# Extra matmuls in the first attention batch, and the gate/value weights' float32 words moved a part behind their halves

## The chip, the core and the metric

One core of a Trainium2 chip runs the whole program. TensorE (PE) multiplies, VectorE (DVE), ScalarE (ACT) and GpSimd (POOL) do the elementwise work, SyncE (SP) issues every DMA. The metric is device time in microseconds, median of 3 runs.

## What is computed

Attention over 4 batches, 8 heads, 576 positions of 64, in two forms that are added; then a gated block and a squared-ReLU block over 2304 tokens.

```python
q_d, k_d, v_d = means of 4 neighbouring positions
out = repeat(sm_attn(q_d, k_d, v_d), 4) + softmax(scale*q@k.T where |i-j| < 4) @ v
x = out as (2304, 512)
xn = x / sqrt(mean(x*x) + 1e-6) * rms_g
x = (silu(xn @ w_gate) * (xn @ w_val)) @ w_out        # 512 -> 1536 -> 512
h = relu(x @ w_in)
y = (s*h*h + b) @ w_out2                              # 512 -> 2048 -> 512
```

The weights come as 64-bit floats, the rest as 32-bit floats.

## The kernel before

A planner (the tile framework) lays out each engine's instructions at build time: it takes instructions by a priority, which follows the order in which the code emits them and can be shifted (`high_priority`), and by a simulated clock. On the chip each engine takes its own list in that order. `issue_after(ins)` makes what is emitted inside it follow `ins` on that engine's list.

**Stages.** Batch 0 of attention runs first, as four units of two heads each (`early_unit`), then the gated block for token blocks 0 and 1 of 288 (`main01`) with attention batch 1 beside it, then the other blocks with batches 2 and 3, then the second block of layers. `attn_batch` starts a new unit of batch 0 every second step and runs `norm` for each half of the batch behind it; the norm's results X16 are what the gate/value products read.

**A unit.** `load_unit` issues nine DMAs on SP. For batch 0 the rows of q and k lie six to a partition; later batches have one row per partition and chunk. `early_unit` turns q and k (L423 for batch 0: a matmul with the identity for each head and chunk; L426 for the others: one transpose for both heads), ACT copies them out of PSUM (L428), then come local scores `sl` with the mask added by a matmul (L440, L444), scores of the means `sd` (L461), softmaxes on DVE and ACT, turns of the weights (`tpl`, `tpd`), and value products `pvd` and `pl`. `sl`, `sd`, `pvd`, `pl` and the turned tiles are each a PSUM tile.

**Weights.** `rest()` emits the preparation of the gated block's weights in steps: for each of four parts (`prep_gv`) eight chunks of 128 x 384, four of w_gate and four of w_val, then two maxima (`st`, L646, L647), scales, and two groups of splits into half-precision pairs. A chunk is fetched by one DMA into staging (`fetch`, L621) and converted to float32 words by two passes on ACT (L624, L625) and two on DVE (L626, L630). The split by DVE (`halves`) is one ACT and one DVE instruction (L127, L128); that by POOL is two POOL instructions with one of ACT between (L130, L131, L132). w_gate is split with DVE, w_val with POOL. After the parts, `weigh` fetches the twelve chunks of w_out, squares them (L666), sums the squares by a matmul `so` (L671), and splits them.

**Where they lie.** `Chain` keeps the words of a chunk 512 columns behind the place of its halves in `W1`, so the halves of one chunk lie on words of the two chunks before it. `Cgv` starts at column 0, `Co` (w_out) at 12288. Staging has four places in `W1` from column 14720 (`ring`), which 28 fetches may use, and two of its own. The loads of three units of batch 0 also lie in `W1`, at 11776, 6656 and 9216.

**Order by hand.** `queued(1)` puts part 1's instructions on ACT and DVE behind the second local softmax of unit 3 (`gates[1]`), `queued(2)` those of parts 2 and 3 and of w_out behind the first half's norm (`gates[2]`). SP, PE and POOL have no such gate. In `main01` each step of the products asks `rest_it` for two further steps; a step of `moe1_gv` is 12 matmuls (`pg` or `pvl`, L708). What `rest_it` has left is emitted before `moe1_out` (`po`, L729).

Of the kernel before, what the change touches and what calls it, by code (L numbers as in the profile page):

```python
# [8 lines left out]
F32 = mybir.dt.float32  # L9
F16 = mybir.dt.float16  # L10
BF16 = mybir.dt.bfloat16
I32 = mybir.dt.int32
# [6 lines left out]
B, H, S, D = 4, 8, 576, 64  # L19
NT, DM, F1, F2 = 2304, 512, 1536, 2048  # L20
NP = H // 2
KC = DM // 128
NF1 = F1 // 128
# [5 lines left out]
GR = 96  # L29
# [10 lines left out]
REST = 2  # L40
RATE0 = 0
EARLY = 2
CAP0 = 100
PDPE = 2
DEP = False
# [1 line left out]
MASKB = 1  # L47
LOADW = (0, 1, 1, 1)
PIN = 0
RING = 4  # L50
RINGN = 28
RESTN = 1
OFF = 0
OFF1 = 0
# [15 lines left out]
def kernel(  # L70
# [46 lines left out]
    Xf = X.rearrange("p k g c -> p k (g c)")  # L117
    X16 = X.bitcast(F16).rearrange("p k g (h c) -> p k g h c", h=2)

    ENG = [(dve, pool)] * NPART + [dve]  # L120

    QB = (dve, dve)
    DEM = pool if DEP else dve
# [28 lines left out]
        def split(self, o, n, scale, eng):  # L152
            halves(self.half(o, n, 0), self.half(o, n, 1), self.f32(o, n), scale, eng)

    Cgv = Chain(W1, 0, 512)
    Co = Chain(W1, 12288, 512)
    C3 = Chain(W1, 0, 512)

# [72 lines left out]
    def load_unit(b, hp, qkf, vd, vw):  # L231
        h0 = 2 * hp
        for t, src in enumerate((q, k)):
            for h in range(2):
                if b == 0:
                    sp.dma_start(out=qkf[:, t, h], in_=src[b, h0 + h].rearrange("(p c) d -> p c d", c=6))
                else:
                    sp.dma_start(out=qkf[:, t, :, h, :], in_=src[b, h0 + h].rearrange("(c p) d -> p c d", p=GR))
        sp.dma_start(out=vd.rearrange("p a r d -> p a (r d)"),
                     in_=v[b, h0:h0 + 2].rearrange("h (t p r) d -> p (h t) (r d)", p=72, r=4))  # L240
        sp.dma_start(out=vw[:, :, 0, :], in_=v[b, h0:h0 + 2, 0:WIN, :].rearrange("h p d -> p h d"))
        sp.dma_start(out=vw[:, :, 8, :], in_=v[b, h0:h0 + 2, S - WIN:S, :].rearrange("h p d -> p h d"))
        for h in range(2):
            base = v[b, h0 + h, 61:62, 0:1]
            sp.dma_start(out=vw[:, h, 1:8, :],
                         in_=bass.AP(tensor=base.tensor, offset=base.offset, ap=[[D, WIN], [64 * D, 7], [1, D]]))
# [94 lines left out]

    LL = ((0, 0), (0, 1), (1, 0))

    def values_d(vdh, PdT, scale, pairs=LL):
        pvd = pV.tile([128, SD], F32, tag="v", name="pvd")
        n_ = 2 * len(pairs) - 1
        for sl, c0, a0, n in ((0, 0, 0, 64), (1, 64, 0, 64), (2, 128, 48, 16)):
            i = 0
            for g in range(2):
                for lv, lp in pairs:  # L350
                    for h in range(2):
                        pe.matmul(out=pvd[64 * h:64 * h + 64, c0:c0 + n], lhsT=vdh[:, lv, 2 * h + g, :],  # L352
                                  rhs=PdT[:72, 6 * lp + 2 * sl + g, 64 * h + a0:64 * h + a0 + n],
                                  start=i == 0, stop=i == n_, skip_group_check=True)
                    i += 1
        od = ap.tile([128, SD], F32, tag="od", name="od", bufs=2)
        act.activation(out=od, in_=pvd, func=AF.Copy, scale=scale)
        return od

    def values_l(b, hp, js, vh, PlT, od, scale, pairs=LL):  # L360
        pl = pV.tile([128, 320], F32, tag="v", name="pl")
        for j in js:
            o = 64 * (j - js[0])
            for i, (lv, lp) in enumerate(pairs):
                for h in range(2):
                    ph = slice(64 * h, 64 * h + 64)
                    pe.matmul(out=pl[ph, o:o + 64], lhsT=vh[:, lv, h, j, :],  # L367
                              rhs=PlT[:WIN, 9 * lp + j, ph], start=i == 0, stop=i == len(pairs) - 1,
                              skip_group_check=True)
        lo, n = 64 * js[0], 64 * len(js)  # L370
        t0 = b * S
        dve.scalar_tensor_tensor(
            out=Xf[:, hp, t0 + lo:t0 + lo + n].rearrange("p (a r) -> p a r", r=4),
            in0=pl[:, :n].rearrange("p (a r) -> p a r", r=4), scalar=scale,
            in1=od[:, lo // 4:(lo + n) // 4].unsqueeze(2).to_broadcast([128, n // 4, 4]),
            op0=ALU.mult, op1=ALU.add)
# [10 lines left out]

    JS = (range(5), range(5, 9))

    def turned(b, n, name):  # L390
        if b == 0:
            return mmp.tile([128, 3, n], F32, tag="mm", name=name)
        return pS.tile([128, 3, n], F32, tag="s", name=name)

    def early_unit(b, hp, sq_sum):
# [17 lines left out]
        qkT = st["qkT"]  # L413
        for t in range(2):
            qT = qkT[:, S * t:S * t + S]
            qT = qT.rearrange("p (a c) -> p c a", c=6) if b == 0 else qT.rearrange("p (c a) -> p c a", c=6)
            for g in range(2):
                tp = turned(b, GR, "tp")
                for i in range(3):
                    c = 3 * g + i  # L420
                    if b == 0:
                        for h in range(2):
                            pe.matmul(out=tp[64 * h:64 * h + 64, i, :], lhsT=qkf[:, t, h, c, :],  # L423
                                      rhs=ident_f[:GR, :GR], start=True, stop=True, skip_group_check=True)
                    else:
                        pe.transpose(out=tp[:, i, :], in_=qkf[:, t, c].rearrange("p h d -> p (h d)"),  # L426
                                     identity=ident_f[:GR, :GR])
                act.activation(out=qT[:, 3 * g:3 * g + 3, :], in_=tp, func=AF.Copy)  # L428
        q4 = qkT.rearrange("p (a r) -> p a r", r=4)
        q2 = st["PlT"][:, :576].rearrange("p (a r) -> p a r", r=2)  # L430
# [5 lines left out]

        def local(js):
            sl = pS.tile([128, 5, WIN], F32, tag="s", name="sl")
            for p0 in (0, 64):
                pe.matmul(out=sl[p0:p0 + 64, :len(js), :], lhsT=ident_b[p0:p0 + 64, p0:p0 + 64],  # L440
                          rhs=mask[p0:p0 + 64, js[0]:js[0] + len(js), :], start=True, stop=False, skip_group_check=True)
            for j in js:
                for p0 in (0, 64):
                    pe.matmul(out=sl[p0:p0 + 64, j - js[0], :], lhsT=qkT[p0:p0 + 64, 64 * j:64 * j + 64],  # L444
                              rhs=qkT[p0:p0 + 64, S + win0(j):S + win0(j) + WIN], start=False, stop=True,
                              skip_group_check=True)
            return sl
# [8 lines left out]

        sl = local(JS[0])
        sd = pX.tile([128, 3, SD], F32, tag="x", name="sd")
        for o, q0 in ((0, 0), (1, 64), (2, SD - 64)):
            for p0 in (0, 64):  # L460
                pe.matmul(out=sd[p0:p0 + 64, o, :], lhsT=qd[p0:p0 + 64, q0:q0 + 64],  # L461
                          rhs=qd[p0:p0 + 64, SD:2 * SD], start=True, stop=True, skip_group_check=True)
# [16 lines left out]
            act.activation(out=PdT[:72, 3 * g:3 * g + 3, :], in_=tp[:72], func=AF.Copy)  # L479
        a = p1.tile([128, TB], F32, tag="u", name="a1", bufs=3)[:, :280].rearrange("p (j k) -> p j k", j=4) if b == 0 else None  # L480
        a = softmax_l(sl, JS[1], 1.0 / 8, 1.0, 1, dve if b == 0 and hp == NP - 1 else pool, a)
        if b == 0 and hp == NP - 1:
            gates[1] = tuple(last)
        yield
        od = values_d(vs.unsqueeze(1), PdT, 0.25, ((0, 0),))
        turn(a, JS[1])
        yield
        values_l(b, hp, JS[0], vw.unsqueeze(1), PlT, od, 1.0, ((0, 0),))
# [77 lines left out]
    def norm(b, hh, sq_sum):  # L566
# [28 lines left out]
            last[:] = (act.activation(out=dst[:, :, 0, :], in_=sv, func=AF.Copy).ins,  # L595
                       eng.tensor_tensor(out=dst[:, :, 1, :], in0=sv, in1=dst[:, :, 0, :], op=ALU.subtract).ins)
        if b == 0 and hh == 0:
            gates[2] = tuple(last)
        yield


    ring = [W1[:, 14720 + 1024 * i:14720 + 1024 * i + 1024].bitcast(I32).rearrange("p (n t) -> p n t", t=2)
            for i in range(RING)]
    fetched = [0]

# [198 lines left out]
    def rest():  # L804
        for p_ in range(NPART + 1):
            it = prep_gv(p_, ENG[p_]) if p_ < NPART else weigh(Co, w_out, NF1, 0, invg, ENG[4], "o")
            while True:
                with queued(min(p_, 2)) if p_ else nullcontext():
                    if next(it, 0) == 0:
                        break  # L810
                yield

    late = [LATE0]

    def later_rest():
        it = rest()
        while True:
            with tc.high_priority(offset=-late[0]):
                if next(it, 0) == 0:
                    return  # L820
            yield

    rest_it = later_rest()
    staged = []
    for hp in range(NP):
        o = (11776, 6656, 9216, 0)[hp]
        if hp < NP - 1:
            st_ = (W1[:GR, o:o + 1536].rearrange("p (t h c d) -> p t h c d", t=2, c=6, h=2),
                   W1[:72, o + 1536:o + 2560].rearrange("p (a r d) -> p a r d", a=4, r=4))
        else:  # L830
            st_ = (ap.tile([GR, 2, 2, 6, D], F32, tag="qkf", name="qkf"),
                   ap.tile([72, 4, 4, D], F32, tag="vd", name="vd"))
        st_ += (early[hp]["vh"][:WIN].rearrange("p (h j d) -> p h j d", h=2, j=NJ),)
        for _ in range(LOADW[hp]):
            next(rest_it)
        load_unit(0, hp, *st_)
        staged.append(st_)
# [47 lines left out]
    for blk in range(NB):  # L885
# [31 lines left out]
        for n, ev_ in enumerate(main(blk) if blk else main01()):  # L917
            if blk == 0:
                if n % RESTN == 0:
                    for _ in range(REST):  # L920
                        next(rest_it, None)
            if n == 1 or ev_ == "post":
                run_posts()
            if side is not None:
# [123 lines left out]
```

## Time and profile before

| | us |
|---|---|
| median of 3 runs | 1107.35 (1106.99 to 1108.79) |
| the profiled execution | 1106.15 |
| its span | 1104.4 |
| PE busy | 1003.6 (91%) |
| DVE, ACT, POOL busy | 592.8, 521.4, 339.5 |

The trace is of one execution. Times in it run from the span's start. [...] A matmul's duration holds its passage through the array, so matmuls that follow each other closely add up to more than the time they take together; the "busy" of a stretch counts such overlap once.

### The profile page before, as it was taken

Reading aid. Unit: us, or ns where it says so; the run is one execution under the profiler, and the core shown is the slowest. Engines: PE = TensorE matmul, PEld = TensorE weight load, DVE = VectorE, ACT = ScalarE, POOL = GpSimd, SP = SyncE. Lnnn points to the kernel's source line nnn. Section 1 sums busy time; section 2 is a strip of 40 time slices with the busy share of each in tenths; the row PEclk is TensorE's granted clock in tenths of the full one; section 3 lists DMA queues with packets and bytes.
Section 4 is the critical chain, followed back from the end, with each engine's and each line's share of the span. In section 5 each row is a group of like instructions: output and inputs, shape, how many; then the busy total and the mean of one; then the engine's idle time right before and its main releaser. Section 6 shows DMA issues by size and latency. Waiting matters only on the chain.

```text
span 1104.4 us, 20466 instructions
## 1 busy us (share of the span) xinstructions
PE 1003.6 (91%) x8204; PEld 685.4 (62%) x8206; DVE 592.8 (54%) x1255; ACT 521.4 (47%) x1174; POOL 339.5 (31%) x433
## 2 busy tenths in 40 slices
PE   5775686899988989898999999999999999999998
PEld 4663564678866767676778667755554545455553
DVE  3766996642187764576762876656341414234241
ACT  3655778643255554355644777756140413223140
POOL 6435674246144545453644213621000000000000
PEclk7675885899988989998999999999999999999999
DMA  8733456100035542145511442400000000000000
GB/s 195 212 87 98 137 156 174 36 20 13 1 67 91 116 88 49 39 84 90 117 38 39 134 134 77 160 32 1 29 1 29 1 20 11 10 20 1 29 1 29
DMA packets 120431, 73.59 MB, mean 67 GB/s; under 512 B 102161, under 2 KB 108305, under 8 KB 120337
## 3 DMA queue, kind: packets, MB, share of 16 engines
q1 hardware_dynamic: 120336, 72.29, 26.1%
q8 instruction: 64, 1.05, 0.4%
q14 instruction: 31, 0.25, 0.1%
HBM read 54.97 MB, written 4.72 MB: 54 GB/s over the span
## 4 chain that ended last, share of the span: by engine, by line
PE 66%; DMA 13%; DVE 10%; ACT 6%; issue 3%; POOL 2%; SPq 1%; DVEq 0%; POOLq 0%; ACTq 0%
PE y L1010 17%; PE ph L990 16%; PE po L729 8%; PE pvl L708 8%; PE pg L708 8%; DMA stg<-in_moe_w_in_dram 3%; DMA qkT<-qk 3%; DMA stg<-in_moe_w_out_dram 2%; DVE W L630 2%; DVE stg L626 2%; DMA vd<-in_v_dram 2%; ACT stg L625 1%; PE pl L367 1%; PE pvd L352 1%; ACT W L624 1%
## 5 line engine op out<-in xcount | busy, mean ns | idle before, releaser
L708 PEld LDWEIGHTS <-W 128*128 128x128 f16 x2304 | 229.1, 101 | 88.9 <-issue 23.9
L990 PE MATMUL ph<-X,W 128*128 128x384 f16 x1152 | 196.6, 326 | 0.4 <-DVE s4o L673 0.3
L708 PE MATMUL pg<-X,W 128*128 128x288 f16 x1152 | 170.2, 296 | 15.0 <-DVE u L715 11.0
L708 PE MATMUL pvl<-X,W 128*128 128x288 f16 x1152 | 172.3, 295 | 0.6 <-DVE m L647 0.5
L990 PEld LDWEIGHTS <-W 128*128 128x128 f16 x1152 | 112.6, 98 | 81.5 <-issue 1.2
L1010 PE MATMUL y<-W 128*128 128x512 f16 x648 | 151.6, 379 | 0.0
L729 PEld LDWEIGHTS <-W 128*128 128x128 f16 x1152 | 111.5, 98 | 31.1 <-issue 2.8
L729 PE MATMUL po<-g,W 128*128 128x288 f16 x1008 | 129.0, 287 | 1.6 <-DVE u L715 0.9
L994 ACT ACTIVATE r<-ph 128x384 f32<-128x384 f32 x96 | 47.0, 490 | 175.8 <-PE ph L990 126.1
L719 POOL TENSOR_TENSOR g<-u,g 128x288 f16<-128x288 f32 x84 | 72.1, 859 | 140.3 <-ACT g L718 106.1
L1010 PEld LDWEIGHTS <-W 128*128 128x128 f16 x648 | 63.4, 98 | 70.9
L190 DVE SCALAR_TENSOR_TENSOR r<-ph,r 128x384 f32<-128x384 f32 x96 | 53.5, 557 | 59.5 <-ACT r L994 59.5
L1015 DVE SCALAR_TENSOR_TENSOR ys<-y,ccol,bcol 128x512 f32<-128x512 f32 x18 | 13.5, 751 | 121.1 <-PE y L1010 118.9
L718 ACT ACTIVATE g<-u 128x288 f16<-128x288 f32 x84 | 36.8, 438 | 77.7 <-DVE u L190 72.6
L715 DVE SCALAR_TENSOR_TENSOR u<-u,pvl 128x288 f32<-128x288 f32 x96 | 42.7, 447 | 45.7 <-PE pvl L708 42.2
L626 DVE SCALAR_TENSOR_TENSOR stg<-stg 128x512 int32<-128x512 int32 (+1 forms) x56 | 42.3, 756 | 35.0 <-ACT stg L625 34.4
L998 DVE TENSOR_TENSOR W<-r,W 128x384 f16<-128x384 f32 x72 | 40.1, 557 | 36.6 <-ACT W L997 36.6
L997 ACT ACTIVATE W<-r 128x384 f16<-128x384 f32 x72 | 37.5, 521 | 39.9 <-DVE r L190 39.9
L714 ACT ACTIVATE u<-pg,tsc 128x288 f32<-128x288 f32 x96 | 47.1, 492 | 16.5 <-PE pg L708 15.7
L1010 PE MATMUL y<-W,r2b 128*128 128x512 f16 x216 | 50.0, 379 | 0.0
L630 DVE SCALAR_TENSOR_TENSOR W<-W,stg 128x512 int32<-128x512 int32 (+1 forms) x56 | 47.9, 857 | 2.9 <-ACT W L624 2.3
L624 ACT ACTIVATE W<-stg 128x512 f32<-128x512 f32 (+1 forms) x56 | 36.0, 645 | 21.0 <-DMA stg<-in_moe_w_out_dram 10.0
(260 smaller groups left out, 1462.1 us busy)
## 6 DMA issues: line engine op xcount, KB each, us to landing
stg<-in_moe_w_out_dram SPq DMA_DIRECT2D x28, 512.0 KB
stg<-in_moe_w_in_dram SPq DMA_DIRECT2D x16, 512.0 KB
W<-in_moe_w_gate_dram SPq DMA_DIRECT2D x12, 384.0 KB
out_dram<-ys SPq DMA_DIRECT2D x18, 256.0 KB
qkf<-in_q_dram SPq DMA_DIRECT2D x26, 144.0 KB
qkf<-in_k_dram SPq DMA_DIRECT2D x26, 144.0 KB
vd<-in_v_dram SPq DMA_DIRECT2D x13, 288.0 KB
W<-in_moe_w_val_dram SPq DMA_DIRECT2D x8, 384.0 KB
```

The costliest lines, as they stand in the source:

```text
L190: (eng or dve).scalar_tensor_tensor(out=o, in0=a, scalar=s, in1=b, op0=ALU.mult, op1=ALU.mult)
L624: act.activation(out=dst, in_=stg[:, :, 1].bitcast(F32), func=AF.Copy, scale=2.0 ** -112)
L626: ins = dve.scalar_tensor_tensor(out=stg[:, :, 0], in0=stg[:, :, 1], scalar=-2 ** 31, in1=stg[:, :, 0], op0=ALU.bitwise_and, op1=ALU.bitwi ...
L630: dve.scalar_tensor_tensor(out=di, in0=di, scalar=3, in1=stg[:, :, 0], op0=ALU.logical_shift_left, op1=ALU.bitwise_or)
L708: pe.matmul(out=acc, lhsT=Cgv.half(o, FP, lw)[:, f0 * 128:f0 * 128 + 128], rhs=X16[:, kc, 3 * blk:3 * blk + 3, lx, :], start=i == 0, stop= ...
L714: act.activation(out=u, in_=ps[0], func=AF.Tanh, scale=tsc[:, part:part + 1])
L715: dve.scalar_tensor_tensor(out=u, in0=u, scalar=1.0, in1=ps[1], op0=ALU.add, op1=ALU.mult)
L719: pool.tensor_tensor(out=lo, in0=u, in1=hi, op=ALU.subtract)
L729: pe.matmul(out=acc, lhsT=Co.half(fc * 512, 512, lw)[:, m * 128:(m + 1) * 128], rhs=g16(fc)[:, lx, :], start=i == 0, stop=i == 35)
L990: pe.matmul(out=acc, lhsT=C2.half((p * KC + kc) * 512, 512, lw)[:, f0 * 128:f0 * 128 + 128], rhs=X16[:, kc, 4 * blk:4 * blk + 4, lx, :], s ...
L994: act.activation(out=r, in_=acc, func=AF.Relu, scale=2.0 ** -23)
L1010: pe.matmul(out=y, lhsT=src[:, lx, tt * 128:(tt + 1) * 128], rhs=C3.half(fc * 512, 512, lw), start=i == 0, stop=i == 47)
```

## The change

- Batch 0 (`WARMB = 1`) gets matmuls whose results nobody reads: after each allocation of a PSUM tile of a unit, `warm` multiplies a matrix of ones by the mask into that tile, 2, 2, 2, 4 or 2 times (turned tiles, `sl`, `sd`, `pvd`, `pl`). The real matmuls then overwrite it.
- The shift of `Cgv` grows from 512 columns to 3072, the words of one part. Staging moves to column 15744, has three places, and 37 fetches may use it.
- Parts 0 and 1 split w_val with DVE instead of POOL.
- Batch 0 loads and turns q and k as the other batches do.
- `gates[1]` is unit 1's second local softmax, `gates[2]` unit 3's, `gates[3]` the norm; part p waits for gate p, w_out for gate 3.
- In `main01` the loop asks for no more than 60 steps of `rest_it` (four parts of 12 and the 12 fetches of w_out).

```diff
+WARMB = 1
+WARM = (2, 2, 2, 4, 2)
-RING = 4
-RINGN = 28
+RING = 3
+RINGN = 37
-    ENG = [(dve, pool)] * NPART + [dve]
+    ENG = [(dve, dve), (dve, dve), (dve, pool), (dve, pool), dve]
-    Cgv = Chain(W1, 0, 512)
+    Cgv = Chain(W1, 0, FP * 8)
@@ load_unit
-                if b == 0:
-                    sp.dma_start(out=qkf[:, t, h], in_=src[b, h0 + h].rearrange("(p c) d -> p c d", c=6))
-                else:
-                    sp.dma_start(out=qkf[:, t, :, h, :], in_=src[b, h0 + h].rearrange("(c p) d -> p c d", p=GR))
+                sp.dma_start(out=qkf[:, t, :, h, :], in_=src[b, h0 + h].rearrange("(c p) d -> p c d", p=GR))
@@ values_d, values_l, local and the tile sd likewise
+            warm(warm_b, pvd, WARM[3])
+        warm(b, pl, WARM[4])
+            warm(b, sl.rearrange("p a b -> p (a b)"), WARM[1])
+        warm(b, sd.rearrange("p a b -> p (a b)"), WARM[2])
+    warm_in = mask.rearrange("p j k -> p (j k)")
+    def warm(b, t, n):
+        if b < WARMB:
+            for _ in range(n):
+                pe.matmul(out=t, lhsT=ones_b, rhs=warm_in[:, :t.shape[1]], start=True, stop=True, skip_group_check=True)
     def turned(b, n, name):
         if b == 0:
-            return mmp.tile([128, 3, n], F32, tag="mm", name=name)
+            t = mmp.tile([128, 3, n], F32, tag="mm", name=name)
+            warm(b, t.rearrange("p a b -> p (a b)"), WARM[0])
+            return t
@@ early_unit
-            qT = qT.rearrange("p (a c) -> p c a", c=6) if b == 0 else qT.rearrange("p (c a) -> p c a", c=6)
+            qT = qT.rearrange("p (c a) -> p c a", c=6)
-                    c = 3 * g + i
-                    if b == 0:
-                        for h in range(2):
-                            pe.matmul(out=tp[64 * h:64 * h + 64, i, :], lhsT=qkf[:, t, h, c, :],
-                                      rhs=ident_f[:GR, :GR], start=True, stop=True, skip_group_check=True)
-                    else:
-                        pe.transpose(out=tp[:, i, :], in_=qkf[:, t, c].rearrange("p h d -> p (h d)"),
-                                     identity=ident_f[:GR, :GR])
+                    pe.transpose(out=tp[:, i, :], in_=qkf[:, t, 3 * g + i].rearrange("p h d -> p (h d)"),
+                                 identity=ident_f[:GR, :GR])
-        if b == 0 and hp == NP - 1:
-            gates[1] = tuple(last)
+        if b == 0 and hp % 2:
+            gates[1 + hp // 2] = tuple(last)
@@ norm
-            gates[2] = tuple(last)
+            gates[3] = tuple(last)
@@
-    ring = [W1[:, 14720 + 1024 * i:14720 + 1024 * i + 1024].bitcast(I32).rearrange("p (n t) -> p n t", t=2)
+    ring = [W1[:, 15744 + 1024 * i:15744 + 1024 * i + 1024].bitcast(I32).rearrange("p (n t) -> p n t", t=2)
@@ rest
-                with queued(min(p_, 2)) if p_ else nullcontext():
+                with queued(min(p_, 3)) if p_ else nullcontext():
@@ the loop over main01
-                        next(rest_it, None)
+                        if steps[0] < 12 * NPART + NF1:
+                            next(rest_it, None)
```

## Rows read from the trace of the kernel before

**Rows 1.** the page's 40 slices: granted TensorE clock and DMA share

```profile
PEclk7675885899988989998999999999999999999999
...
DMA  8733456100035542145511442400000000000000
```

**Rows 2.** busy time by stretch: PE, PEld, DVE, ACT, POOL, PEclk, DMA share, GB/s

```profile
0.00:93.00 93.00, 64.33 (x781) 52.92 (x781) 54.49 (x121) 49.02 (x126) 44.33 (x71) 0.72 0.67 168
...
104.60:158.00 53.40, 43.28 (x379) 32.35 (x378) 49.08 (x108) 39.37 (x96) 30.39 (x35) 0.90 0.42 127
...
158.00:197.00 39.00, 24.51 (x190) 17.83 (x191) 28.15 (x47) 29.14 (x76) 18.64 (x19) 0.52 0.60 168
...
197.00:264.00 67.00, 66.86 (x600) 50.48 (x600) 34.34 (x82) 35.42 (x84) 28.98 (x39) 0.95 0.08 20
...
178.00:186.00 8.00, 7.91 (x58) 5.70 (x58) 3.68 (x8) 6.32 (x18) 3.26 (x4) 0.50 0.50 151
...
4.00:24.00 20.00, 14.79 (x157) 12.55 (x157) 5.20 (x13) 6.98 (x13) 10.70 (x19) 0.81 0.99 220
...
54.30:60.50 6.20, 5.92 (x111) 4.75 (x109) 2.53 (x8) 2.56 (x8) 2.21 (x3) 1.00 0.85 196
```

**Rows 3.** PE in order of time, 154 to 200 us: start, us, instructions

```profile
154.97 1.63 PE L708 MATMUL pvl<-X,W 128*128 128x288 f16 x12
...
197.14 0.17 PE L671 MATMUL so<-abo,ones_b 128*128 128x12 bf16 x1 [3.41 <-POOL abo L669]
...
197.16 3.04 PE L708 MATMUL pg<-X,W 128*128 128x288 f16 x12
```

**Rows 4.** the chain that ended last, in order of time: start, us, what

```profile
197.31 2.89 PE pg L708 x12
...
251.19 1.47 PE pg L708 x12
```

**Rows 5.** the gate product, 197 to 264 us (the value product has as many)

```profile
L708 PE MATMUL pg<-X,W x180: 286/286/448, 197.2 to 262.4; 128*128 128x288 f16 x180
```

**Rows 6.** POOL in order of time

```profile
8.33 0.24 POOL L179 TENSOR_SCALAR_AFFINE_SELECT mask<-mask 64x70 bf16<-64x70 bf16 x1
...
190.73 0.91 POOL L132 TENSOR_TENSOR W<-W 128x384 f16<-128x384 f32 x1 [0.63 <-ACT W L131]
```

**Rows 7.** who SP's queue waited for, 0 to 200 us: us, times, longest

```profile
SPq L621 <- DVE W L630: 106.4, 31, 18.4
```

**Rows 8.** DVE in order of time

```profile
143.54 0.55 DVE L630 SCALAR_TENSOR_TENSOR W<-W,stg 128x384 int32<-128x384 int32 x1
...
222.88 0.75 DVE L128 SCALAR_TENSOR_TENSOR W<-W,sgo 128x512 f16<-128x512 f32 x1
```

**Rows 9.** groups of ACT instructions, 0 to 93 us: count, busy, mean ns

```profile
L624 ACT ACTIVATE W<-W 128x384 f32<-128x384 f32 x12 | 6.3, 544 | 12.0 <-DMA W<-in_moe_w_gate_dram 8.4 <-DMA W<-in_moe_w_val_dram 3.5
```

**Rows 10.** who waited for POOL's last split step (L132), 80 to 200 us: us, times

```profile
  ACT W L131: 6.3, 3
```

**Rows 11.** groups of DVE instructions, 93 to 264 us

```profile
L128 DVE SCALAR_TENSOR_TENSOR W<-W,rs 128x384 f16<-128x384 f32 x12 | 7.8, 652 | 5.9 <-ACT W L127 5.9
```

**Rows 12.** groups of POOL instructions, 94 to 103 us

```profile
L130 POOL TENSOR_TENSOR W<-W,rs 128x384 f32<-128x384 f32 x4 | 3.2, 826 | 0.2 <-DVE invg L190 0.2
...
L132 POOL TENSOR_TENSOR W<-W 128x384 f16<-128x384 f32 x3 | 2.7, 908 | 0.0
```

**Rows 13.** ACT in order of time

```profile
144.94 0.68 ACT L624 ACTIVATE W<-stg 128x512 f32<-128x512 f32 x1
```

**Rows 14.** PE in order of time, first batch

```profile
5.32 4.48 PE L423 MATMUL tp<-ident_f,W 96*64 96x96 f32 x48 [0.34 <-POOL mask L177]
...
68.50 0.69 PE L426 MATMUL tp<-ident_f,qkf 96*128 96x96 f32 x3
```

**Rows 15.** groups of ACT copies out of turned tiles, 0 to 93 us

```profile
L428 ACT ACTIVATE gx<-tp 128x288 f32<-128x288 f32 x4 | 2.7, 682 | 0.0
```

**Rows 16.** the same, 93 to 264 us

```profile
L428 ACT ACTIVATE P_l<-tp 128x288 f32<-128x288 f32 x8 | 3.2, 404 | 0.7 <-PE tp L426 0.7
```

More of the change, by code (lines that the diff above doesn't have):

```diff
@@ L342, with values_d @@
     LL = ((0, 0), (0, 1), (1, 0))
-    def values_d(vdh, PdT, scale, pairs=LL):
+    def values_d(vdh, PdT, scale, pairs=LL, warm_b=None):
         pvd = pV.tile([128, SD], F32, tag="v", name="pvd")
+        if warm_b is not None:
+            warm(warm_b, pvd, WARM[3])
         n_ = 2 * len(pairs) - 1
@@ L481, in early_unit @@
         a = softmax_l(sl, JS[1], 1.0 / 8, 1.0, 1, dve if b == 0 and hp == NP - 1 else pool, a)
-        if b == 0 and hp == NP - 1:
-            gates[1] = tuple(last)
+        if b == 0 and hp % 2:
+            gates[1 + hp // 2] = tuple(last)
         yield
-        od = values_d(vs.unsqueeze(1), PdT, 0.25, ((0, 0),))
+        od = values_d(vs.unsqueeze(1), PdT, 0.25, ((0, 0),), b)
         turn(a, JS[1])
@@ L813 @@
     late = [LATE0]
+    steps = [0]
     def later_rest():
@@ L820, in later_rest @@
                     return
+            steps[0] += 1
             yield
@@ L827 @@
         if hp < NP - 1:
-            st_ = (W1[:GR, o:o + 1536].rearrange("p (t h c d) -> p t h c d", t=2, c=6, h=2),
+            st_ = (W1[:GR, o:o + 1536].rearrange("p (t c h d) -> p t c h d", t=2, c=6, h=2),
                    W1[:72, o + 1536:o + 2560].rearrange("p (a r d) -> p a r d", a=4, r=4))
         else:
-            st_ = (ap.tile([GR, 2, 2, 6, D], F32, tag="qkf", name="qkf"),
+            st_ = (ap.tile([GR, 2, 6, 2, D], F32, tag="qkf", name="qkf"),
                    ap.tile([72, 4, 4, D], F32, tag="vd", name="vd"))
```

## The prediction

> **What bounds the kernel now.** I first read the page's slices [rows 1]: TensorE's granted clock holds at 8 or 9 tenths from the eighth slice (193 us) on; before that it swings between 5 and 8, and the DMA engines, busy at 8 and 7 tenths for two slices (55 us), fall to 3 to 6 while weights are still to be loaded. So the loss lies in the first fifth of the span. The table by stage shows it [rows 2]: in 0 to 93 us (first batch of attention) PE is busy for 64.3 us at a clock of 0.72; in 104.6 to 158 for 43.3 of 53.4; in 158 to 197 for 24.5 of 39 at 0.52; in 197 to 264 for all but 0.1 us at 0.95. Everything the change touches is done by 264 us, where the first block's output product begins. What comes after is PE work that nothing here alters.
>
> The third view is PE in order of time around 158 us [rows 3]. The gate/value product stops at 156.6 us, and its next matmul starts at 197.16, 0.02 us after `so`, a matmul of 12 columns that sums the squares of w_out. PE takes its instructions in order, so a product whose operands may long have been there stood behind a sum that waits for the last of w_out's twelve chunks. That first product then runs cold: 2.89 us for 12 matmuls against 1.47 at full clock [rows 4].
>
> How large is the loss between the first product (104.6) and 264? 2 blocks x 12 column groups x 2 x 12 = 576 matmuls at 1.47/12 = 0.1225 us are 70.6 us; 360 of them lie behind 197 [rows 5]. Other PE work, at full clock: in 197 to 264, 66.9 - 360 x 0.1225 = 22.8; in 104.6 to 158, 43.3 - 216 x 0.1225 = 16.8; in 158 to 197, 24.5 at half clock, an estimate of 13. Together 123 of 159.4 us: **36 us are lost**, 24.6 of them idle (10.1 before 158, 14.5 behind it), the rest cold.
>
> **The change part by part.** *`so` moved.* With `steps[0] < 60` the loop asks for w_out's loads but not for `so`, the scale and the splits; they are emitted after all 576 products of blocks 0 and 1. This removes PE's blockade at 158 to 197: 14.5 us idle and 11.5 cold. It is worth that only if the weights are there. Until now the queue on PE hid that part 3 was ready only when POOL ended its last split, at 191.6 [rows 6].
>
> *Gates and shift.* The wait for free staging is SP's largest: 106.4 us up to 200 us [rows 7]. Staging is freed by DVE's two conversion passes (0.55 us each, the last gate/value one ending at 144.1 [rows 8]) beside two on ACT (0.54 each [rows 9]); part 1's stand behind unit 3's second softmax, part 2's behind the norm. The change puts them behind unit 1's and unit 3's. So part 2's eight chunks, 8 x 1.1 = 8.8 us of DVE and 8.6 of ACT, leave the stage after the norm, where DVE is busy for 49.1 of 53.4 us [rows 2]. Queued behind the new waits are the steps of units 2 and 3 and the norm, on ACT and DVE. With one chunk of shift a split writes over the float32 words of its neighbours, so each waits for the one before (ACT waited 6.3 us in three waits for POOL's last step [rows 10]); with a part of shift they are independent. The price: part 3's words now reach column 15360, so w_out's first five chunks (words from 12800) wait for part 3's splits, where before they did not. Staging falls from 4 + 2 to 3 + 2 slots, but the ring serves 37 fetches, not 28; against SP's 106 us I cost that at nothing, up to 2 us either way.
>
> When is part 3 ready then? Its conversions no longer stand behind part 2's: 9 to 15 us sooner than 144; I take 130. Maximum and scale I put at 8 us, four gate splits at 4 x 1.3 (0.65 on DVE [rows 11] and about as long on ACT), four value splits on POOL at 4 x 1.75 (0.83 + 0.91 [rows 12]): some 150 with the two kinds one after the other, 148 if they overlap a little, instead of 191.6. From w_out's first conversion to its last split it took 144.9 [rows 13] to 223.6 [rows 8], 78.7 us. At that pace the output product starts at 148 + 78.7 = 227. PE's own floor is 104.6 + 123 = 228. Two bounds at one place will not both be met; I take back four fifths of the 26 us lost behind 158 (20 us), half of the 10 us idle before it (5 us), and leave the rest.
>
> *The head.* POOL did seven weight steps, 3.2 + 2.7 = 5.9 us, between the norm's first and last step [rows 12]; parts 0 and 1 split on ACT and DVE now. That gives up to 5 us and costs DVE 8 x 0.65 = 5 us, most of them before the norm, where DVE is idle for 38 of 93 us [rows 2]; were it not, the 5 us would be lost again. The transposes fall from 48 matmuls a unit to 12 (one for both heads). The first unit's 48 took 4.48 us; of the new form three took 0.69, twelve thus 2.8 [rows 14]: up to 7 us of PE in four units. ACT's copy out of them, contiguous now, takes 404 ns instead of 682 [rows 15, 16]: 16 x 0.28 = 4.5 us. Against it: the loads of q and k now come in rows of 256 bytes instead of 1536. The old pattern moved 220 GB/s (4 to 24 us), a later unit that loads with the new pattern 196 [rows 2]: 2.36 MB take 12.0 instead of 10.7 us, 1.3 us more; bounds 0 and 5 us.
>
> *Useless matmuls.* 34 in each unit, with 8 x 288 + 8 x 384 + 4 x 384 + 4 x 350 + 2 x 432 + 4 x 144 + 4 x 320 = 11,032 columns; four units 44,128. By the product's row (288 columns in 0.1225 us) that is 18.8 us at full clock, by the cold one (2.89/12) 36.9. PE's idle time up to 93 us is 28.7. At full clock they fit, and the real work shortens: 64.3 us at a mean of 0.72. The gain on the path is bounded by 0 and some 8 us, since most waits here are for ACT, DVE and loads. One cost is plain: they read `mask`, which POOL finishes at 8.57 us [rows 6], while the first transposes start at 5.32 [rows 14]; standing ahead of them on PE they shift unit 0 by up to 3.3 us. Sum of the head: 5 + 4 - 1.3 - 3.3, the matmuls at 0, is about +4; with as many in-order queues between these and the norm I take 1 us of it.
>
> **Sum.** 20 + 5 + 1 = 26 us off the profiled execution's 1106.15 (span 1104.4 and 1.75 around it): 1080. The median of the runs is 1.2 higher: **1081 us**. With the bounds above (head -10 to +8, the stage behind it 17 to 36) the forecast's own range is 1063 to 1100.
>
> **The rivals.** *The clock stays low* (1094 us). In 178 to 186 us PE was busy for 7.91 of 8 us, with transposes between value products, and the granted clock was 0.50, the lower level, throughout [rows 2]. If the first batch's narrow work stays there, the useless matmuls cost 36.9 us against 28.7 idle, PE becomes the bound of the head, and with waits that it can't fill the head ends up to 13 us later: 1081 + 13. [...]
>
> *w_out behind part 3* (1104 us, hardly to be told from no change). If part 3 is ready at 175 to 185 us instead of 148, w_out's 78.7 us end at 254 to 264, where the output product started before: 0 to 10 us are won. For it speaks that 47 us passed from the last gate/value conversion to part 3's last split; against it, that this was waiting in queues more than work.
>
> *Slower: weights ahead of attention* (1113 us). The place is ACT and DVE between 45 and 93 us. The gates let 16 conversions of 1.1 us on ACT and 1.1 on DVE into in-order queues before units 2 and 3 and the norm are through: 16 x 2.2 = 35 us if all of it stands ahead of them and nothing overlaps, 28 with a fifth overlapped. The head ends that much later, and against the 26 gained that is 2 to 9 us slower. It decides from 26 us on: a first product later than 131 us. Against it: DVE and ACT are idle for 38 and 44 of 93 us [rows 2] and can take the words in the gaps.
>
> *The floor* (1060 or less): all 36 us and 8 of the head come back.
>
> **How the numbers follow.** Forecast 0.60, low clock 0.12, w_out 0.08, slower 0.15, floor 0.05. About 0.2% (2.2 us) is what a measurement can tell from no change. Faster: forecast, low clock and floor, 0.77; same 0.08; slower 0.15. The range leaves out the slower rival and the far side of the floor: 1060 to 1108.
>
> **What would show it.** Right: `so` stands behind the last gate/value product or close to it on PE; no stretch like 158 to 197; part 2's conversions before the norm; POOL's norm steps without weight steps between; the output product at 232 to 245 us; the clock above 0.72 in 0 to 93. Wrong: the first product after 110 us, a clock near 0.6 in the head, the first w_out conversion after 170, or a new wait of PE for w_out's splits. Work after the output product should be the same, only earlier; if the span moves by much more or less than that start, a later stage has been reordered and my sum misses it.

## The result, and the profile after

| | before | after |
|---|---|---|
| median of 4 runs each | 1107.64 (1106.99 to 1108.79) | 1067.26 (1064.92 to 1070.0) |
| ratio, 95% interval | | 0.9635 (0.961 to 0.966) |
| profiled execution, span | 1106.15, 1104.4 | 1066.8, 1065.1 |
| first gate product `pg` | 104.60 | 93.14 |
| output product `po` | 264.07 | 217.84 |

40.4 us are gone by the medians, 39.3 by the spans; the forecast was 26. The measured 1067.26 lies within the forecast's range of 1063 to 1100, near its lower end. In the changed kernel the same work has other line numbers: `fetch` L629, its last conversion pass L638, splits L129 and L130 (ACT, DVE) and L132 and L134 (POOL), `so` L679, products L716, `po` L737, useless matmuls L398, transposes L432, their copies L434.

The page's slices of after, granted TensorE clock in tenths of full speed and DMA share (26.6 us each): two slices below 9 are left in the first fifth, the third at 8 and the fourth at 6 (80 to 107 us, where the norm stands), against the eight slices at 5 to 8 of [rows 1]; the DMA engines stay at 9, 9 and 8 tenths for the three slices before it.

```profile
PEclk9986999999988899999999999999999999999999
DMA  9985144010345430555312424300000000000000
```

The table by stage of after (stretch, length, then busy us and instruction count of PE, PEld, DVE, ACT, POOL, then clock, DMA share, GB/s):

```profile
0.00:93.00 93.00, 69.18 (x791) 49.38 (x792) 70.86 (x161) 58.40 (x154) 46.48 (x74) 0.89 0.85 205
93.10:145.00 51.90, 46.63 (x388) 35.48 (x388) 48.28 (x101) 38.32 (x91) 34.49 (x39) 0.94 0.28 95
145.00:180.00 35.00, 34.98 (x316) 26.32 (x314) 21.70 (x47) 25.82 (x69) 11.41 (x14) 1.00 0.47 141
180.00:205.00 25.00, 25.00 (x222) 18.36 (x223) 9.60 (x24) 9.40 (x27) 8.70 (x11) 0.93 0.20 49
```

Nothing like the 39 us at 0.52 of [rows 2] is left: from 145 to 205 us PE is busy throughout, at 1.00 and 0.93. In the first batch DVE is busy 16 us longer and ACT 9 us longer than before, and the stage ends 11.5 us sooner all the same: weight work has moved into their gaps there.

PE of after in order of time (start, busy us, instructions, idle time before in brackets):

```profile
8.03 0.64 PE L398 MATMUL tp<-mask,ones_b 128*128 128x288 bf16 x2 [3.06 <-POOL mask L181]
8.46 0.68 PE L432 MATMUL tp<-ident_f,W 96*128 96x96 f32 x3
...
83.18 1.12 PE L578 MATMUL ssn<-ones_f,sqsum 128*96 128x1 f32 x6 [2.03 <-POOL sqsum L388]
89.19 0.26 PE L594 MATMUL rb<-ident_b,rp 96*128 96x96 bf16 x1 [4.89 <-POOL rp L587]
...
93.14 0.40 PE L716 MATMUL pg<-X,W 128*128 128x288 f16 x1 [1.09 <-ACT X L603]
...
213.41 0.17 PE L679 MATMUL so<-abo,ones_b 128*128 128x12 bf16 x1
213.44 0.90 PE L716 MATMUL pvl<-X,W 128*128 128x288 f16 x6
...
217.84 1.64 PE L737 MATMUL po<-g,W 128*128 128x288 f16 x12
```

`so` now stands at the end of the products and waits for nothing. The stage from the first product to `po` fell from 159.5 to 124.7 us. 6.9 us of those 34.8 are no gain: after 217.84 PE still does the last scores, turns and value products of attention batch 1 (0.95 + 0.71 + 0.96 + 1.01 + 1.10 + 0.63 + 1.49 us in the same view), which before were done when `po` began. 11.5 + 34.8 - 6.9 = 39.4, the difference of the spans.

Two more views of after: who SP's queue waited for up to 200 us (us, times, longest), and POOL's last split steps of w_val (count, ns least/median/most, first and last start). Against [rows 6, 7] the largest wait fell from 106.4 to 88.2 us, and the last of these steps starts at 138.4 us instead of 190.73.

```profile
SPq L629 <- DVE W L638: 88.2, 30, 26.6
```

The last split steps of w_val on POOL:

```profile
L134 POOL TENSOR_TENSOR W<-W x8: 902/1067/1364, 123.8 to 138.4; 128x384 f16<-128x384 f32 x8
```

### The profile page after: what moved, and what is told of

Same layout as the page of the kernel before. It is cut to its first block, busy times and chain, and to the rows that moved or that the text cites. A ratio compares the mean times of both kernels' runs of the same rounds, so it can differ in the third digit from the quotient of the medians.

```text
span 1065.1 us, 20448 instructions
## 1 busy us (share of the span) xinstructions
PE 988.2 (93%) x8198; PEld 668.0 (63%) x8198; DVE 597.1 (56%) x1263; ACT 517.0 (49%) x1174; POOL 323.9 (30%) x417
## 4 chain that ended last, share of the span: by engine, by line
PE 62%; DVE 14%; DMA 12%; ACT 5%; issue 4%; POOL 2%; SPq 1%; DVEq 0%; POOLq 0%; ACTq 0%
PE y L1021 18%; PE ph L1001 17%; PE po L737 8%; PE pg L716 7%; PE pvl L716 6%; DMA stg<-in_moe_w_in_dram 3%; DMA stg<-in_moe_w_out_dram 2%; DMA qkT<-qk 2%; DMA PlT<-P_l 2%; DVE W L638 2%; DVE stg L634 2%; PE pl L369 1%; DMA PdT<-P_d 1%; ACT stg L633 1%; DVE W L130 1%
## 5 line engine op out<-in xcount | busy, mean ns | idle before, releaser
L716 PEld LDWEIGHTS <-W 128*128 128x128 f16 x2304 | 227.5, 100 | 83.9 <-issue 20.7
L716 PE MATMUL pg<-X,W 128*128 128x288 f16 x1152 | 169.8, 295 | 9.5 <-DVE u L723 8.5
L716 PE MATMUL pvl<-X,W 128*128 128x288 f16 x1152 | 167.8, 292 | 4.8 <-DVE u L192 3.0
L737 PEld LDWEIGHTS <-W 128*128 128x128 f16 x1152 | 112.1, 99 | 36.2 <-issue 7.0
L737 PE MATMUL po<-g,W 128*128 128x288 f16 x1008 | 132.5, 289 | 1.0 <-POOL g L727 0.7
L192 DVE SCALAR_TENSOR_TENSOR u<-u,pg 128x288 f32<-128x288 f32 x96 | 43.1, 449 | 1.7
```

The costliest lines, as they stand in the source:

```text
L192: (eng or dve).scalar_tensor_tensor(out=o, in0=a, scalar=s, in1=b, op0=ALU.mult, op1=ALU.mult)
L716: pe.matmul(out=acc, lhsT=Cgv.half(o, FP, lw)[:, f0 * 128:f0 * 128 + 128], rhs=X16[:, kc, 3 * blk:3 * blk + 3, lx, :], start=i == 0, stop= ...
L737: pe.matmul(out=acc, lhsT=Co.half(fc * 512, 512, lw)[:, m * 128:(m + 1) * 128], rhs=g16(fc)[:, lx, :], start=i == 0, stop=i == 35)
```

## The experiments

Each stood beside its own runs of before; ratios are to be compared. After itself gave 0.9635 at first and 0.9676 in a later comparison, so that differences under some 4.5 us between rows of this table say nothing, except within one comparison of many runs. "Pays" is what its part is worth in after by the medians, against 1067.3 and 1070.4 (the last two rows: in before). `pg` and `po` are starts in the one profiled execution of each row; of the first row there is a second, below.

| kernel | median | ratio (95%) | first `pg` | `po` | the part pays |
|---|---|---|---|---|---|
| after without useless matmuls | 1070.9 | 0.9681 (0.9643 to 0.9719) | 91.80 | 216.49 | 0 to 4 (0.5 within one comparison) |
| ... without the bound of 60 | 1085.0 | 0.9811 (0.9785 to 0.9837) | 93.52 | 244.62 | 15 to 18 |
| ... with the old gates | 1079.4 | 0.9758 (0.973 to 0.9785) | 89.78 | 223.52 | 9 to 12 |
| ... with the old shift and ring | 1069.6 | 0.9658 (0.9634 to 0.9683) | 86.14 | 221.22 | -1 to 2 |
| ... with w_val's splits on POOL | 1080.4 | 0.9755 (0.9731 to 0.9779) | 102.17 | 231.12 | 10 to 13 |
| ... with the old loads and turns | 1086.6 | 0.9804 (0.9783 to 0.9825) | 108.76 | 232.92 | 16 to 19 |
| before with the bound of 60 | 1079.3 | 0.9769 (0.9723 to 0.9816) | 105.50 | 235.73 | 27 in before (20 to 31 by the interval) |
| before with useless matmuls | 1105.4 | 0.9983 (0.9968 to 0.9999) | 105.12 | 263.81 | 1.5 in before |

### The bound on the steps, taken away and alone

```diff
-                        if steps[0] < 12 * NPART + NF1:
-                            next(rest_it, None)
+                        next(rest_it, None)
```

> The changed kernel without the bound of 60 steps, so that the sum of w_out's squares (so) is emitted within the products again, as before. Theory (the bound removed PE's blockade): so stands ahead of the products of part 1's second block on PE, PE does only attention from some 120 us until w_out's last square (about 167 us), and the output product starts 15 to 30 us later than 217.8: 1082 to 1097 us. Rival (with earlier gates the weights come in time, and so blocks nothing that matters): 1065 to 1070 us.

PE of this kernel in order of time:

```profile
138.84 0.91 PE L716 MATMUL pvl<-X,W 128*128 128x288 f16 x6
...
173.31 0.19 PE L679 MATMUL so<-abo,ones_b 128*128 128x12 bf16 x1
173.36 1.12 PE L716 MATMUL pg<-X,W 128*128 128x288 f16 x4
```

The table by stage:

```profile
139.00:174.00 35.00, 22.89 (x190) 16.79 (x189) 21.55 (x43) 26.97 (x71) 12.43 (x15) 0.53 0.59 173
```

The picture of [rows 3] is back, 24 us earlier: the products stop, `so` comes 34 us later, the next product 0.05 us behind it, and the clock is 0.53 in between. The weights of part 3 were ready at 140.7 here (POOL's last step at 139.7), so it isn't they that the products waited for. `po` begins 26.8 us later than in after, the span is only 18.9 longer: attention batch 1's last matmuls, which after does behind the start of `po`, are done ahead of it here.

The converse, before with that one edit (and the counter `steps` that it needs):

```diff
+                        if steps[0] < 12 * NPART + NF1:
+                            next(rest_it, None)
-                        next(rest_it, None)
```

> The kernel before with the bound of 60 steps alone. Theory (so's place on PE is the largest part of the gain, and part 3's readiness at 191.6 us limits it here): the products go on at 158 us with parts 1 and 2, and the output product starts 15 to 22 us earlier than 264: 1085 to 1092 us. Rival (without earlier weights the moved sum is worth nothing, PE then waits for part 3 or for w_out): 1100 to 1108 us.

27.3 us by the medians (25.6 by the ratio, 20 to 31 by its interval), at the upper end of the expected 15 to 22 or above it. POOL's last split step in this kernel:

```profile
194.20 0.91 POOL L132 TENSOR_TENSOR W<-W 128x384 f16<-128x384 f32 x1
```

PE:

```profile
231.15 0.18 PE L671 MATMUL so<-abo,ones_b 128*128 128x12 bf16 x1
235.73 3.57 PE L729 MATMUL po<-g,W 128*128 128x288 f16 x24 [0.55 <-ACT W L127]
```

The stretch 158 to 197:

```profile
158.00:197.00 39.00, 36.71 (x319) 27.49 (x317) 31.83 (x57) 33.84 (x88) 21.59 (x25) 0.96 0.52 161
```

Part 3 was ready no sooner than before (195.1 us against 191.6 [rows 6]), and yet PE was busy for 36.7 of 39 us at 0.96, on products of the earlier parts that had stood behind `so`. `po` began 40.6 us after part 3 was ready. So it was not part 3's readiness that held PE from 158 to 197 us in before, but the place of one matmul of 12 columns, which waited for the last of w_out's chunks.

### The old loads and turns

```diff
+                if b == 0:
+                    sp.dma_start(out=qkf[:, t, h], in_=src[b, h0 + h].rearrange("(p c) d -> p c d", c=6))
...
+                    if b == 0:
+                        for h in range(2):
+                            pe.matmul(out=tp[64 * h:64 * h + 64, i, :], lhsT=qkf[:, t, h, c, :],
+                                      rhs=ident_f[:GR, :GR], start=True, stop=True, skip_group_check=True)
```

> The changed kernel with batch 0's q and k loaded in rows of 1536 bytes and turned head by head with the identity again. Theory (48 more matmuls a unit, and ACT's copies at 0.68 instead of 0.40 us, lengthen the head): first product 3 to 7 us later than 93.1, 1070 to 1075 us. Rival (the loads in rows of 256 bytes cost what the turns save): 1065 to 1069 us, the DMA share of 0 to 40 us below 0.95.

(The tiles' layouts change with it. A unit's turns are 48 matmuls in the trace instead of 12, so 36 more, not 48 more.) 16 to 19 us, far more than was expected. The first product came at 108.76 instead of 93.14, and that in the fastest of its five executions (1077.84 of 1077.84 to 1089.56), the one that was profiled. The stretch 0 to 40 us, of after and then of this kernel, and a group of its copies on ACT, 0 to 93 us (busy us, mean ns):

```profile
0.00:40.00 40.00, 32.36 (x326) 22.46 (x327) 20.28 (x49) 19.41 (x54) 25.26 (x50) 1.00 0.95 209
```

```profile
0.00:40.00 40.00, 29.30 (x240) 17.82 (x240) 13.03 (x31) 15.43 (x35) 20.76 (x45) 0.91 0.91 208
```

Its copies:

```profile
L443 ACT ACTIVATE gx<-tp 128x288 f32<-128x288 f32 x4 | 2.8, 700 | 0.3 <-PE tp L438 0.3
```

Together with v and the weights, 209 GB/s were moved with rows of 256 bytes and 208 with rows of 1536. The DMA engines were busy for 0.95 instead of 0.91 of the 40 us for it, 1.6 us more, near the 1.3 that I had put on the short rows; but as many bytes arrived, so it delayed nothing that these rows show. The rival's sign (a share below 0.95) came, its time did not. Three of the four groups of copies take 696 to 706 ns again and the fourth 550 at the mean, against 404 to 408 in after. Fewer matmuls, shorter copies and the order that the planner builds around them were changed together; which of them makes the 15.6 us wasn't separated. Most of it arises early: the last turn of the three units whose q and k lie in `W1` starts at 30.9 us in after and at 43.8 here.

The rival that the useless matmuls only make up for the cost of the old form was tested by leaving out both (the edits of this kernel, which the next lines call e6, and `WARMB = 0`):

> The changed kernel with the old loads and turns and without useless matmuls. Theory (the old form costs by its own matmuls and copies): the first product still 6 or more us later than 93.1, 1074 to 1086 us. Rival (it cost 19 us in e6 only because useless matmuls stand before four times as many real ones on PE): first product at 91 to 96 us, 1066 to 1071 us.

1096.5 (1093.5 to 1099.1), ratio 0.9908 (0.9888 to 0.9928), first product at 113.45: the old form costs 25.6 us against after without useless matmuls in the same comparison (1070.9). The theory held, with a larger size; and beside the old form the useless matmuls are worth some 10 us (1096.5 against 1086.6, from different comparisons, and the second with a wide spread; `po` at 245.2 against 232.9). In before, which has the old form too, they bring 1.5 (below); what makes the difference was not settled.

### Who splits w_val

```diff
-    ENG = [(dve, dve), (dve, dve), (dve, pool), (dve, pool), dve]
+    ENG = [(dve, pool)] * NPART + [dve]
```

> The changed kernel with w_val of parts 0 and 1 split with POOL again. Theory (POOL's weight steps stood between the norm's steps; this is what made the first product 11.5 us earlier): first product at 98 to 104 us, time 1072 to 1078 us. Rival (with the words a part apart and earlier, POOL's steps fall outside the norm): first product at 92 to 95 us, 1065 to 1069 us.

POOL between the norm's steps in this kernel, in order of time:

```profile
93.97 1.20 POOL L583 TENSOR_TENSOR r<-ms,mhalf 96x3 f32<-96x3 f32 x1
95.15 3.50 POOL L134 TENSOR_TENSOR W<-W 128x384 f16<-128x384 f32 x4
98.74 0.23 POOL L585 TENSOR_SCALAR r<-r 96x3 f32<-96x3 f32 x1
99.04 0.19 POOL L587 CAST rp<-r 96x3 bf16<-96x3 f32 x1
```

PE:

```profile
99.28 0.26 PE L594 MATMUL rb<-ident_b,rp 96*128 96x96 bf16 x1 [12.63 <-POOL rp L587]
```

The norm's first POOL step comes 8.4 us after the sum of squares (`ssn`, 85.53 us): `ms` on DVE stands behind splits until 91.08, and then POOL is at weight steps until 93.97. Its second waits behind four weight steps; PE waits 12.6 us. In after no weight step stands there; on DVE:

```profile
86.75 0.15 DVE L582 TENSOR_SCALAR ms<-ssn 96x3 f32<-96x3 f32 x1
```

and on POOL:

```profile
86.98 1.26 POOL L583 TENSOR_TENSOR r<-ms,mhalf 96x3 f32<-96x3 f32 x1 [0.63 <-DVE ms L582]
88.33 0.32 POOL L585 TENSOR_SCALAR r<-r 96x3 f32<-96x3 f32 x1
88.72 0.42 POOL L587 CAST rp<-r 96x3 bf16<-96x3 f32 x1
```

But the wait has a successor. `ssn` began at 83.18, and `ms` on DVE came 3.6 us later, behind splits:

```profile
81.86 2.74 DVE L130 SCALAR_TENSOR_TENSOR W<-W,rs 128x384 f16<-128x384 f32 x4
...
87.42 3.78 DVE L130 SCALAR_TENSOR_TENSOR W<-W,rs 128x384 f16<-128x384 f32 x7
```

Of the 10 to 13 us, 9.0 show in the first product (102.17 against 93.14): 2.4 ahead of `ssn`, 7.7 from there to `rb`, less 1.1 behind it. POOL's queue is not the whole of it. DVE's gate/value splits took 1.14 us each at the median in this kernel, many of them beside POOL's weight steps, against 0.61 in after; how the 9.0 divide between the two wasn't separated.

### The gates, and the shift

```diff
-        if b == 0 and hp % 2:
-            gates[1 + hp // 2] = tuple(last)
+        if b == 0 and hp == NP - 1:
+            gates[1] = tuple(last)
@@ norm
-            gates[3] = tuple(last)
+            gates[2] = tuple(last)
@@ rest
-                with queued(min(p_, 3)) if p_ else nullcontext():
+                with queued(min(p_, 2)) if p_ else nullcontext():
```

> The changed kernel with the gates of before: part 1's conversions behind unit 3's softmax, parts 2, 3 and w_out behind the norm. Theory (earlier gates carry the stage behind the norm): part 3 is ready 12 to 20 us later than 139.6 us, PE waits for parts 1 and 2, the output product starts 8 to 15 us later: 1074 to 1082 us. The head could be 2 to 4 us shorter, since fewer conversions lie in it. Rival (PE had slack because so no longer blocks it): 1065 to 1070 us.

The head is 3.4 us shorter with the old gates and `po` 5.7 us later, with POOL's last step of part 3 starting at 147.6 instead of 138.4: what the weights gain outweighs it. The earlier gates buy the weights at the price of the head. The time came as the theory said, its parts smaller, since another 8.9 of the 14.6 us between the profiled executions (1081.38 and 1066.8) lie behind `po`, in the first block's later stages (485 us from `po` to the first `y` in after, 494 here). What makes them longer was not settled.

```diff
-RING = 3
-RINGN = 37
+RING = 4
+RINGN = 28
-    Cgv = Chain(W1, 0, FP * 8)
+    Cgv = Chain(W1, 0, 512)
@@
-    ring = [W1[:, 15744 + 1024 * i:15744 + 1024 * i + 1024].bitcast(I32).rearrange("p (n t) -> p n t", t=2)
+    ring = [W1[:, 14720 + 1024 * i:14720 + 1024 * i + 1024].bitcast(I32).rearrange("p (n t) -> p n t", t=2)
```

> The changed kernel with the gate/value words one chunk (512 columns) behind their halves again, and staging as before (four places from column 14720, 28 fetches). Theory (splits in a chain hold each other up, and with them what stands behind them on ACT and DVE): the first product 2 to 5 us later than 93.1, part 3 ready 5 to 15 us later than 139.6, time 1071 to 1080 us. Rival (the shift's price, w_out waiting for part 3, is as large as its gain): first product the same, w_out's first conversion earlier than 133 us, 1062 to 1068 us.

POOL's last split steps of w_val in this kernel:

```profile
L134 POOL TENSOR_TENSOR W<-W x8: 906/912/915, 141.9 to 177.9; 128x384 f16<-128x384 f32 x8
```

PE:

```profile
86.14 0.40 PE L716 MATMUL pg<-X,W 128*128 128x288 f16 x1 [1.09 <-ACT X L603]
...
221.22 1.65 PE L737 MATMUL po<-g,W 128*128 128x288 f16 x12 [0.30 <-ACT W L129]
```

The shift does what it says: with it part 3's last POOL step starts at 138.4, without it at 177.9. It is worth 0 to 2 us all the same. The head is 7 us shorter without it, with one split of DVE ahead of `ms` instead of eight, and the 40 us by which part 3 is late cost hardly anything, as in the kernel above where it was ready at 195.

### The useless matmuls

Left out of after:

```diff
-WARMB = 1
+WARMB = 0
```

> The changed kernel with the useless matmuls left out (WARMB = 0), all else kept. Theory (they pay through the clock): the granted clock of the head falls from 0.89 in 0 to 93 us towards the 0.72 of before, real PE work there stretches, the first gate/value product comes 4 to 8 us later than 93.1 and the time is 1071 to 1076 us. Rival (they fill waits that are for other engines, and cost the 3 us in which they wait for the mask): the first product comes at 90 to 94 us and the time is 1063 to 1068.

1070.9 (1066.5 to 1074.1), between the two forecasts; the first product came at 91.80, as the rival said, at a clock of 0.77.

Before with them alone (`WARMB`, `WARM`, `warm` and its calls of the change's diff, nothing else):

> The kernel before with the useless matmuls alone. Theory (they shift the head by the wait for the mask and their own time, and the clock they win is not on the path): granted clock of 0 to 93 us up from 0.72 to 0.85 or more, first product at 104 to 110 us, time 1105 to 1114 us. Rival (the head's PE work on the path runs faster): first product 4 to 8 us earlier, 1098 to 1103 us.

The theory held: 1105.4, first product at 105.12, clock 0.92.

After, with another operand that needs no `mask`:

```diff
-                pe.matmul(out=t, lhsT=ones_b, rhs=warm_in[:, :t.shape[1]], start=True, stop=True, skip_group_check=True)
+                pe.matmul(out=t, lhsT=ones_b, rhs=ones_b[:, :1].to_broadcast([128, t.shape[1]]), start=True, stop=True, skip_group_check=True)
```

> The changed kernel whose useless matmuls read a broadcast column of the matrix of ones instead of the mask, so that they do not wait for POOL's mask (to 8.57 us). Theory (that wait costs unit 0 about 3 us, most of it lost among other waits): the first transposes at 5 to 6 us instead of 8.5, the first product 0 to 2 us earlier than 93.1, 1064 to 1068 us. Rival (constant data changes the granted clock, or the wait was hidden): clock of the head off 0.89 by more than 0.05, or the same time within 2 us.

The last gave 1071.4 (1062.7 to 1074.0), ratio 0.9659 (0.9616 to 0.9702): `ssn` comes 5 us earlier (78.19) and the first product 2.9, so the wait for `mask` does lengthen the head; but `po` comes at 220.7, later than 217.84, and the time is the same. This decides nothing. Since the first left an interval of 8 us, after and after without useless matmuls were set side by side in more runs, neither edited further:

> The changed kernel once more, beside the one without useless matmuls on the same chip: 1065 to 1070 us by both theories. The first product at 93.1, the output product at 217.8 us as before, since the program is the same.

> The changed kernel without useless matmuls, with more rounds. Theory now (they raise the head's clock but not its end, since the head waits for other engines; first product at 91.8 against 93.1): within 0.3% of the changed kernel, ratio to the kernel before 0.962 to 0.968. Rival (they pay 3 to 4 us): ratio 0.003 or more above that of the changed kernel on the same chip, with intervals apart.

After 1070.4 (1068.7 to 1073.5), without 1070.9 (1067.3 to 1073.6), ratios 0.9676 (0.9658 to 0.9694) and 0.967 (0.9648 to 0.9692). Stretches 0 to 93 us of after without them (second comparison) and of before with them:

```profile
0.00:93.00 93.00, 63.85 (x658) 49.31 (x659) 69.40 (x163) 58.35 (x155) 45.41 (x74) 0.67 0.83 205
```

```profile
0.00:93.00 93.00, 74.75 (x917) 51.64 (x918) 53.18 (x119) 47.94 (x123) 44.41 (x70) 0.92 0.66 168
```

They do raise the clock, from 0.77 and 0.67 to 0.89 and 0.92 in after (two profiled executions each) and from 0.72 to 0.92 in before, and PE's busy time with it; the median moves by nothing in after and by 0.17% in before. The execution at 0.67 (1072.61) was 3.9 us longer than the one at 0.92 in the same comparison (1068.70), but not in the head: its first product came 0.6 us earlier, its `po` 5.0 us later (221.4 against 216.4).

## Why the prediction was right in its direction and 14 us short

**`so` moved: the step held, its size failed.** I let the removal count only as far as part 3's weights were ready, and took 20 of 26 us, and half of the 10 us idle before 158. Before with the bound alone gave 27, with part 3 ready at 195. The wrong step is to count the weights as there only when part 3 is: products of earlier parts were waiting behind `so`, enough for PE until part 3 came. The pace of 78.7 us from w_out's first conversion to its last split wasn't a bound either: `po` starts before all splits are done (after: the last on DVE starts at 236.6, `po` at 217.84). For the same reason the forecast of 148 us for part 3 was good (139.5) and mattered little. 124.7 us for the stage look like PE's own floor of 123, but 6.9 us of work were moved behind it. So by my own measure 27.9 of the 36 us were won, not 25, and some 8 are still lost. The sign that I gave, `po` at 232 to 245, was missed at 217.84.

**The head: mis-sized, 1 us taken, 11.5 measured.** I had 5 for POOL, 4 for the copies, and took nearly all back for in-order queues. Single removals show 9.0 for POOL's splits and 15.6 for loads and turns in the first product's start, less 3.4 and 7.0 that gates and shift take away. The discount had no row behind it, and 11.5 lies outside my own bound of +8: of the 13.4 us that the sum fell short of the spans' 39.4, 10.5 are the head's and 2.9 the stage's. That the total still fell within the range owes to the room up to the stage's bound of 36. The result is nearer the floor (1060), to which I gave 0.05, than the forecast. Why the head gained more than its steps' sum is argued and not shown: its chain runs through PE, ACT, DVE and POOL in turn, so shorter steps in each unit can add up. The 1.3 us for shorter rows show as time of the DMA engines, not in the data's arrival.

**Useless matmuls at 0: held, for after and before.** The wait for `mask` is there (3.06 us, first useless matmul at 8.03; 2.9 us of the first product in the run without it); their columns fit PE's idle time, and the clock came out above 0.72. So the low-clock rival fell by its condition. What the useless matmuls would cost at a low clock no run shows; without them, 0.77 and 0.67 in the head did not make its end later. Against a general 0 stands the pair with the old loads, where they bring some 10 us. Without useless matmuls the first batch ran at 0.67 and 0.77 with transposes, in two executions of one program, and at 0.72, 0.74 and 0.80 with identity matmuls. So no run here shows that the form of the turns moved the clock.

**The slower rival** (weights ahead of attention) exists, in small: heads 3.4 and 7.0 us shorter with old gates or shift, and eight of DVE's splits in front of `ms` where the old shift has one. It decided nothing; the first product came at 93, not 131.

**The later stages** moved with `po` except for the 6.9 us, and the span of after shows no other change. They are not fixed, though: with the old gates they took 8.9 us more.

**What doesn't add up.** Single removals from after cost 50 to 64 us in sum, the whole change gains 36 to 40; the bound alone gives 27 of these and the rest together 9 to 13 more, about the head's 11.5. So parts pay more beside the others than alone. One reason is seen: with the bound gone, PE stops at `so` although part 3's weights are ready. That with a late head the weights' time matters less is argued, not shown. That each kernel gets other lists from the planner adds to this; how much is open.

## What to carry to other kernels

Look first at which tiny instruction stands in an in-order queue ahead of much ready work: here moving one reduction of 12 columns gave about 27 of 40 us, and needed no faster weights. Before discounting a gain on a chain that passes through several engines, look for the row that would take it back. A raised clock need not be worth anything: 0.89 or 0.92 instead of 0.67 to 0.77 in the head moved the medians of these two kernels by less than 0.2% within one comparison, so look first whether the others wait for PE there.

## What the runs showed of the hardware that was not expected

POOL's steps of 96x3 elements took longer with DVE's splits beside them. In after the five casts and products from 88.72 on (L587, L589) take 0.42 to 0.46 us each, 2.2 in all, while DVE does seven splits from 87.42 to 91.20; in the kernel with w_val on POOL, where DVE is idle from 97 to 101 us, the same five take 0.18 to 0.19, 0.9 in all. So 1.3 us of what the norm gained on POOL went back to slower steps. Within one run, with the old gates, the steps beside DVE's splits took 0.42 to 0.46 us and the one at 87.71, just behind their end at 87.59, took 0.18. DVE's splits took longer beside POOL's steps, too: in the kernel with w_val on POOL the three from 81.51 to 85.89 took 0.95 to 1.16 us each, with POOL busy without a pause from 78.86 to 86.66, and a split took 1.14 at the median; in after it was 0.61.

The granted clock of the same program differed between executions: after without useless matmuls had 0.77 and 0.67 in 0 to 93 us, with first products at 91.80 and 92.47.
